# Squared-ReLU attention and an FFN on one core: the first two batches' keys in tiles of 128

## The chip, the core and the metric

The kernel runs on one core of a Trainium2 chip. Its engines are TensorE (PE in the profile), VectorE (DVE), ScalarE (ACT), GpSimd (POOL) and SyncE (SP, which here only starts DMAs). Each works through its own queue in order; semaphores tie the queues together. Sixteen DMA engines move data. The metric is the device time of one execution in microseconds (us), as a median of several runs. The kernel before takes 531.14 us (median of 6 runs, 529.06 to 533.16).

## The reference

Eight batches, twelve heads, 448 tokens, head size 64:

```python
scores = scale * q @ k.T                  # per batch and head, 448 x 448
attn   = np.maximum(scores, 0.0) ** 2 / S
x      = (attn @ v)                       # heads side by side: 448 x 768
xn     = (x - mean(x)) / sqrt(var(x) + 1e-6) * g_ln
out    = x + np.maximum(xn @ w_ch1, 0.0) @ w_ch2      # 768 -> 3072 -> 768
```

There is no softmax: a score tile is only clipped at zero and squared, so the keys of a head may be cut in any way and in any order, as long as values and scores are cut alike.

## The kernel before

Work goes by *pairs* of heads (six a batch, numbered 0 to 47 over all batches, `NPAIR` = 6). For a pair, q and k are transposed (`att_T`), so that the head dimension lies on the partitions; a score *slot* `(i, t)` is the scores of both heads of pair `i` for the `t`-th group of keys (`att_QK`, lines 241 to 268): one matmul per head into one of two PSUM buffers `sc`, one ScalarE activation (ReLU, line 268) into a bf16 tile, and one VectorE product that squares it (line 271). The value product (`att_AV`, line 278) sums over the four groups of keys, and VectorE evacuates it as xT (line 298). For batch 0 VectorE also multiplies it with the gains into xc (line 302); this is what the notes call the norm vector.

**Two layouts of keys.** Batches 2 to 7 read their keys as three groups of 128 (`NF` = 3 per partition row) and one of 64. The last 64 keys of two neighbouring pairs share one slot (line 249 on): four matmuls of 64 rows by 64 columns (line 254), each head in its half of the partitions. Values lie accordingly in `v_heads` and in `v_rest`, which is zero where the other head's keys stand. Two pairs then take seven slots. Their q and k are turned by DMA transposes that SyncE starts (line 226). Batches 0 and 1 (`PE_T` = 2) have four groups of 112 keys, eight slots for two pairs, and are transposed on TensorE (`pe_T`, line 208), since w2 and the transposing queue are not free yet.

**The order** is written out by hand. Loads of q, k, v and w1 are issued from GpSimd's queue (lines 737 to 747). Then come six `step_fine` (line 582), one for each pair of batch 0: slots, the value product of the pair before in two halves, the transposes of the next pair, the mean over features of xT (`mean_part`, line 311), and `warm_up` matmuls (line 532) on zeros. `first_end` finishes batch 0's attention and begins pair 6; `ffn_1_first` centers (line 334) and starts the first FFN product. `ffn_1_all` runs the 24 row blocks of that product (line 368), two PSUM banks in turn, and puts *excursions* between them: up to three slots of the next batch's attention, with the third slot's ReLU on VectorE (line 266) in spare banks, and one value product of a pair that is ready. For batch 0 the excursions follow the table `IN_FIRST`, the transposes `T_IN_FIRST`, the statistics of x (lines 359 to 361, on x_tok, which SyncE makes by DMA transposes in line 348) `STATS_AT`; the second entry of `STATS_AT` holds for all later batches. `ffn_2_first` is batch 0's second product (line 413): sixteen parts, tile after tile in one bank each, evacuated in line 399; between the parts stand the gains (line 314) and the centering for batch 1, `carry` (line 379) and the sums of w2 blocks (line 195). Later batches use seven block products instead of eight (`seven`, line 430, with VectorE sums in line 424 and GpSimd sums in line 464).

All loads of later batches (lines 146 to 148, 156, 160) also go through GpSimd's queue, in the order in which they are written, each as soon as the ring buffer it writes to is free.

Of the kernel before, what the change touches and what calls it, by code (L numbers as in the profile page):

```python
# [11 lines left out]
def kernel(  # L12
# [10 lines left out]
    nc = tc.nc  # L23
# [77 lines left out]
    nc.vector.memset(warm, 0.0)  # L101

# [19 lines left out]
    early = w2[:, B_SUM:].rearrange("p a k d -> p (a k d)")[:SP, :4 * EARLY]  # L122
    early = early.rearrange("p (n h e) -> p n h e", n=4, h=H)
    v1_sb = s_sb.rearrange("p a k d -> p (a k d)")[:SP, :EARLY].rearrange("p (h e) -> p h e", h=H)
    v0_sb = v_ring[:SP].rearrange("p (h e) -> p h e", h=H)
    first_qkv = {0: (early[:, 0], early[:, 1], v0_sb), 1: (early[:, 2], early[:, 3], v1_sb)}

    def load_heads(b, pieces):
        pairs = dict(zip("qkv", zip(first_qkv[b], (q, k, v))))
        for name, h0, hs in pieces:  # L130
            sb, src = pairs[name]
            nc.gpsimd.dma_start(
                sb[:, h0:h0 + hs, :],
                src[b, h0:h0 + hs].rearrange("h (p j) d -> p h (j d)", j=NJ))
# [15 lines left out]
    v_heads = v_ring[:, :H * NF * D].rearrange("p (h e) -> p h e", h=H)  # L150
    v_rest = v_ring[:, H * NF * D:].rearrange("p (a e) -> p a e", a=NPAIR)

    def load_v(i):

        b, a = divmod(i, NPAIR)
        nc.gpsimd.dma_start(v_heads[:, 2 * a:2 * a + 4],
# [6 lines left out]
    def v_of(i):  # L163
        b, a = divmod(i, NPAIR)
        return first_qkv[b][2][:, 2 * a:2 * a + 2]

    def load_early():
        q_sb, k_sb, _ = first_qkv[0]
        casts = []
        for sb, src, eng, r0, cast in ((q_sb, q, nc.sync, 0, nc.vector.tensor_copy),  # L170
                                       (k_sb, k, nc.scalar, 6, nc.scalar.copy)):
            st = h[:SP, r0:r0 + 2, :].rearrange("p a t -> p (a t)").bitcast(fp32)
            st = st[:, :2 * NJ * D].rearrange("p (h e) -> p h e", h=2)
            eng.dma_start(st, src[0, :2].rearrange("h (p j) d -> p h (j d)", j=NJ))
            casts.append((cast, sb[:, :2, :], st))
        for cast, dst, st in casts:
            cast(dst, st)
        with nc.allow_non_contiguous_dma(reason="768 gains, once"):
            nc.sync.dma_start(g_sb, moe_g_ln.rearrange("(ko kp) -> kp ko", kp=P))
# [20 lines left out]
    def bf_view(bank):  # L200
        return bank[:, :S].bitcast(bf16).rearrange("p (t s) -> p t s", t=2)

    def pe_T(i, t, ps):
        b, pr = divmod(i, NPAIR)
        sb = first_qkv[b][t]
        for j in range(NJ):
            for hh in range(2):
                nc.tensor.transpose(  # L208
                    ps[hh * D:(hh + 1) * D, t, j * SP:(j + 1) * SP],
                    sb[:, 2 * pr + hh, j * D:(j + 1) * D],  # L210
                    identity[:SP, :SP])
# [4 lines left out]

    def q_of(i, r):
        return qkT[i][r, :NJ, :SP]

    def by_j(x):  # L220
        return x.rearrange("p (j s) -> p j s", j=NJ)

    def att_T(i, copy=None):
        if i >= PE_T * NPAIR:
            new_qkT(i)
            nc.sync.dma_start_transpose(qkT[i], qk_ring[:, i % 3].rearrange("p j c -> p (j c)"))
            return
        if i == 0:
            new_qkT(0)
            for t, cp in enumerate((nc.vector.tensor_copy, nc.scalar.copy)):  # L230
                ps = bf_view(next_f())
                pe_T(0, t, ps)
                cp(qkT[0][:, t * NJ:(t + 1) * NJ, :SP], by_j(ps[:, t, :]))
# [4 lines left out]
        new_qkT(i)  # L238
        (copy or nc.vector.tensor_copy)(qkT[i][:, :, :SP], ps.rearrange("p t (j s) -> p (t j) s", j=NJ))  # L239

    def att_QK(i, t, relu_by=nc.scalar):

        full = attn_pool.tile([P, 2, S], bf16, tag="attn")
        keys = SP if i < PE_T * NPAIR else P
        at = full[:keys]
# [556 lines left out]
```

## Time and profile before

| | us |
|---|---|
| median of 6 runs | 531.14 |
| the profiled execution | 529.06 |
| its span on the core | 527.3 |
| TensorE busy in the span | 519.2 |
| VectorE / ScalarE / GpSimd busy | 377.6 / 277.0 / 217.1 |
| VectorE busy from 10 to 30 | 19.2 of 20 |
| ScalarE busy from 10 to 30 | 18.7 of 20 |
| batch 0's attention ends, centering starts | 30.05 |
| first FFN product, batch 0 | 30.79 to 70.3 |
| second FFN product, batch 0 | 70.3 to 87.1 |
| first FFN product, batch 1 / batch 2 | 87.1 to 127.4 / 155.0 to 192.8 |
| last w1 chunk / last w2 chunk landed | 53.75 / 76.88 |

In the profile a line of a timeline gives start, length, engine, source line, operation and shapes; `x2` means two instructions merged, and brackets give the idle time before them with what ended it. A matmul's length contains its way through the array, so lengths overlap: what a step costs TensorE is the distance to the next start. The chain of waits is followed back from the last instruction to what released each step. The DMA engines are busy without a gap from 4 us to 77 us, at about 200 GB/s.

### The profile page before, as it was taken

The numbers are of one execution on the slowest core, as the hardware profiler recorded it, in microseconds if no ns is written. First come the engines' busy times: TensorE is split into PE (matmuls) and PEld (weight loads), VectorE is DVE, ScalarE is ACT, GpSimd is POOL, SyncE is SP. The second block draws the span as 40 slices with busy tenths as digits, with TensorE's granted clock in tenths as the row PEclk, the third lists the DMA queues.
The fourth block names the chain that finished last, engine by engine and source line by source line (L and its number), as shares of the span: only waits on it lengthen the run. The fifth ranks groups of instructions, "written<-read, shape, count | busy, mean of one in ns | idle before, by whom it ended". The sixth has DMA issues, their size and how long they took to land.

```text
span 527.3 us, 13742 instructions
## 1 busy us (share of the span) xinstructions
PE 519.2 (98%) x5723; PEld 316.1 (60%) x5723; DVE 377.6 (72%) x667; ACT 277.0 (53%) x449; POOL 217.1 (41%) x248
## 2 busy tenths in 40 slices
PE   8999999999999999999999999999999999999996
PEld 4445566556875566655666556655666556665665
DVE  4967889695858868589684886788695876960265
ACT  6956662787227662266623666366624765234320
POOL 9425128377522665227732277228732000320021
PEclk9999999999999999999999999999999999999999
DMA  9999999999637994579924699469924300250022
GB/s 150 196 194 208 204 191 134 192 118 97 73 87 97 110 89 67 129 73 105 112 50 109 73 114 142 83 64 117 104 59 109 46 17 3 69 114 1 1 62 61
DMA packets 171246, 53.04 MB, mean 101 GB/s; under 512 B 145072, under 2 KB 171184, under 8 KB 171184
## 3 DMA queue, kind: packets, MB, share of 16 engines
q0 software_dynamic: 99744, 25.74, 53.4%
q1 hardware_dynamic: 70944, 26.03, 27.0%
q8 instruction: 44, 0.72, 0.6%
q10 hardware_dynamic: 496, 0.40, 0.2%
q14 instruction: 18, 0.15, 0.1%
HBM read 51.91 MB, written 11.01 MB: 119 GB/s over the span
## 4 chain that ended last, share of the span: by engine, by line
PE 94%; DMA 2%; ACT 2%; DVE 1%; issue 0%; DVEq 0%; ACTq 0%
PE f L368 39%; PE f L430 34%; PE f L291 7%; PE sc L259 5%; PE f L413 3%; PE f L259 1%; DMA x_tok<-xT 1%; ACT full L268 1%; PE f L208 1%; PE sc L254 1%; DMA h<-in_k_dram 1%; PE f L627 1%; PE f L532 1%; PE f L327 1%; ACT h L370 0%
## 5 line engine op out<-in xcount | busy, mean ns | idle before, releaser
L368 PE MATMUL f<-xc,w 128*64 128x448 bf16 x2256 | 227.3, 354 | 0.3
L368 PEld LDWEIGHTS <-w 128*64 128x64 bf16 x2256 | 124.9, 110 | 94.0 <-issue 19.4
L370 ACT ACTIVATE h<-f 128x448 bf16<-128x448 f32 x188 | 102.5, 545 | 99.2 <-PE f L368 97.9
L430 PE MATMUL f<-w,s_sb 128*64 128x384 bf16 (+2 forms) x1584 | 130.0, 324 | 0.0
L268 ACT ACTIVATE full<-sc 128x896 bf16<-128x896 f32 (+1 forms) x126 | 108.1, 916 | 15.2 <-PE sc L259 12.5
L430 PEld LDWEIGHTS <-s_sb 128*64 128x64 bf16 x1584 | 92.5, 110 | 34.8
L271 DVE TENSOR_TENSOR full<-full 128x896 bf16<-128x896 bf16 (+1 forms) x174 | 98.7, 617 | 6.9 <-ACT full L268 6.7
L464 POOL TENSOR_TENSOR o_t<-o_t,x_tok 128x384 f32<-128x384 f32 x26 | 24.4, 938 | 152.5 <-ACT o_t L463 132.0
L146 POOL DMA_DIRECT2D qk_ring<-in_q_dram x36 | 48.1, 1338 | 87.5 <-DMA qkT_t<-qk_ring 83.7
L266 DVE TENSOR_SCALAR full<-f 128x448 bf16<-128x448 f32 (+1 forms) x89 | 51.5, 617 | 22.1 <-PE f L259 22.1
L463 ACT ACTIVATE o_t<-f,rstd 128x384 f32<-128x384 f32 x26 | 15.1, 581 | 94.8 <-DVE acc L468 46.8
L424 DVE TENSOR_TENSOR s_sb<-h 128x1536 bf16<-128x1536 bf16 x65 | 64.8, 1013 | 0.0
L147 POOL DMA_DIRECT2D qk_ring<-in_k_dram x36 | 57.2, 1590 | 6.1 <-DMA w<-in_moe_w_ch_dram 6.1
L430 PE MATMUL f<-w,h 128*64 128x384 bf16 x624 | 52.9, 326 | 0.0
L148 POOL DMA_DIRECT2D qk_ring<-in_k_dram x36 | 49.5, 1375 | 7.4 <-DMA w<-in_moe_w_ch_dram 7.4
L298 DVE TENSOR_SCALAR xT<-f 128x448 bf16<-128x448 f32 x43 | 26.7, 622 | 28.5 <-PE f L291 26.6
L430 PEld LDWEIGHTS <-h 128*64 128x64 bf16 x624 | 36.7, 110 | 14.4
L291 PE MATMUL f<-full,v_ring 128*64 128x448 bf16 (+1 forms) x336 | 40.6, 354 | 0.7 <-DVE full L271 0.6
L464 POOL TENSOR_TENSOR acc<-acc,x_tok 128x384 f32<-128x384 f32 x24 | 28.1, 1177 | 22.8 <-ACT acc L463 21.8
L259 PE MATMUL sc<-qkT_t 64*128 64x448 bf16 (+1 forms) x228 | 35.5, 365 | 0.3 <-DVE qkT_t L239 0.2
L160 POOL DMA_DIRECT2D v_ring<-in_v_dram x36 | 33.0, 1239 | 5.2 <-DMA w<-in_moe_w_ch_dram 5.0
L334 DVE SCALAR_TENSOR_TENSOR xc<-f,g_sb,xc 128x448 bf16<-128x448 f32 x48 | 30.2, 677 | 6.0 <-PE f L327 6.0
(75 smaller groups left out, 376.8 us busy)
## 6 DMA issues: line engine op xcount, KB each, us to landing
w<-in_moe_w_ch_dram POOLq DMA_DIRECT2D x6, 768.0 KB, 23.4
w<-in_moe_w_ch_dram POOLq DMA_DIRECT2D x4, 1152.0 KB, 33.7
qk_ring<-in_q_dram POOLq DMA_DIRECT2D x36, 112.0 KB, 5.0
qk_ring<-in_k_dram POOLq DMA_DIRECT2D x36, 96.0 KB, 5.3
v_ring<-in_v_dram POOLq DMA_DIRECT2D x18, 192.0 KB, 5.1
out_dram<-o_t SPq DMA_DIRECT2D x9, 168.0 KB, 2.2
out_dram<-o_t SPq DMA_DIRECT2D x9, 144.0 KB, 2.1
out_dram<-acc SPq DMA_DIRECT2D x7, 144.0 KB, 2.1
```

The lines of the kernel that those rows point to most:

```text
L147: nc.gpsimd.dma_start(k_to[:, :NF], k[b, heads, :SF].rearrange("x (p t) d -> p t x d", t=NF))
L148: nc.gpsimd.dma_start(k_to[:SS, NF], k[b, 2 * a:2 * a + 2, SF:].rearrange("x s d -> s x d"))
L259: nc.tensor.matmul(by_j(half[hh]), qkT[i][r, NJ + t, :keys], q_of(i, r), start=True, stop=True)
L266: nc.vector.tensor_scalar(at[:, x], half[x], 0.0, None, op0=Alu.max)
L268: nc.scalar.activation(at, ps[:keys, :, :S], Act.Relu)
L271: nc.vector.tensor_mul(attn[i, t], attn[i, t], attn[i, t])
L291: nc.tensor.matmul(ps[hh * D:(hh + 1) * D, :], weights, values, start=(t == 0), stop=(t == NJ - 1))
L368: nc.tensor.matmul(ps[c * D:(c + 1) * D, :], w1[:, ki, n0:n0 + D], xc[:, ki, :], start=(ki == 0), stop=(ki == K1 - 1))
L370: nc.scalar.activation(h[:, ni, CARRY:], ps, Act.Relu)
L424: nc.vector.tensor_tensor(s_sb[:, n], x, y, op=op)
L430: nc.tensor.matmul(ps[c * D:(c + 1) * D, :d1 - d0], stat[:, ki, c * D:(c + 1) * D], w2[:, slot, ki, d0:d1], start=(start and ki == 0), sto ...
L464: nc.gpsimd.tensor_tensor(o_t, o_t, x_half(m, dh), op=Alu.add)
```

## The change

Batches 0 and 1 get the key layout of the other six: three groups of 128 and a shared slot for the last 64 keys of two pairs. Queries keep their four groups of 112. Transposes stay on TensorE. Loads split accordingly into a main part, a `k last` and a `v last`; the zeros of `v_rest` are written by VectorE at the start. `step_fine` now covers two pairs, the loads of w1 chunks 2 to 5 and of the rest of batch 1 move between the steps (`load_next`), and the numbers of warm-up matmuls differ. The product with the gains runs on GpSimd for the first four pairs of batch 0. `IN_FIRST` shrinks to six excursions of three slots behind a first one of one slot; the last value product of batch 1's attention comes before the second FFN product instead of inside it. `ffn_2_first` goes through two tiles at once, half by half. Batch 1's statistics stand at row blocks 15, 18, 21 and 23 instead of 6, 9, 12 and 15.

```diff
+    nc.vector.memset(v_ring[:, H * NF * D:], 0.0)
+    v1_sb = s_sb.rearrange("p a k d -> p (a k d)")[:, :H * NJ * D]
+    nc.vector.memset(v1_sb[:, H * NF * D:], 0.0)
...
+            elif name == "k":
+                nc.gpsimd.dma_start(first_k[b][:, heads, :NF].rearrange("p h t d -> p h (t d)"),
+                                    k[b, heads, :SF].rearrange("h (p t) d -> p h (t d)", t=NF))
+            elif name == "k last":
+                nc.gpsimd.dma_start(first_k[b][:SS, heads, NF], k[b, heads, SF:].rearrange("h s d -> s h d"))
+            elif name == "v":
+                nc.gpsimd.dma_start(v_heads[:, heads], v[b, heads, :SF].rearrange("h (p t) d -> p h (t d)", t=NF))
+            elif name == "v last":
+                for e in range(4):
+                    r0 = row0(e // 2, e % 2)
+                    nc.gpsimd.dma_start(v_rest[r0:r0 + SS, e // 2::2, r0:r0 + D],
+                                        v[b, e::4, SF:].rearrange("g s d -> s g d"))
...
         if b == 0:
-            nc.vector.tensor_scalar(xc[:, pr, :], xT_of(b, pr), g_sb[:, pr:pr + 1], None, op0=Alu.mult)
+            eng = nc.gpsimd if pr < NPAIR - 2 else nc.vector
+            eng.tensor_scalar(xc[:, pr, :], xT_of(b, pr), g_sb[:, pr:pr + 1], None, op0=Alu.mult)
...
     def step_fine(i):
+
         att_QK(i, 0)
-        if 0 < i < NPAIR - 1:
-            att_T(i + 1)
-        elif i > 0:
-            warm_up(4)
+        att_T(i + 1)
         att_square(i, 0)
         att_QK(i, 1)
         att_square(i, 1)
-        if i == 0:
-            att_T(1)
+        if i:
+            att_AV(i - 1, 0)
             warm_up(1)
         else:
-            att_AV(i - 1, 0)
+            warm_up(4)
         att_QK(i, 2)
-        if i == 0:
-            warm_up(4)
-        else:
+        if i:
             att_AV(i - 1, 1)
-        att_square(i, 2)
-        att_QK(i, 3)
-        att_square(i, 3)
-        if i > 1:
             mean_part(i - 2)
-            warm_up(2)
         else:
             warm_up(4)
+        att_square(i, 2)
+        att_QK(i, NF)
+        att_square(i, NF)
+        if i:
+            warm_up(4)
+            mean_part(i - 1)
+        else:
+            warm_up(5)
+        att_QK(i + 1, 0)
+        if i + 2 < NPAIR:
+            att_T(i + 2)
+        else:
+            warm_up(5)
+        att_square(i + 1, 0)
+        load_next()
+        att_QK(i + 1, 1)
+        att_square(i + 1, 1)
+        att_AV(i, 0)
+        warm_up(1)
+        att_QK(i + 1, 2)
+        att_AV(i, 1)
+        att_square(i + 1, 2)
+        warm_up(1)
 
     def first_end():
         i = NPAIR
+        mean_part(i - 2)
         att_AV(i - 1, 0)
         att_T(i, nc.scalar.copy)
-        mean_part(i - 2)
...
         for t in range(2):
             att_square(NPAIR, t)
+        excursion(1)
...
-    IN_FIRST = {4: 2, 6: 3, 9: 3, 12: 3, 15: 3, 18: 3, 20: 3, 22: 2}
-    T_IN_FIRST = {5: 1, 8: 2, 11: 3, 14: 4, 17: 5}
+    IN_FIRST = (5, 8, 11, 14, 17, 20)
+    T_IN_FIRST = {4: 1, 7: 2, 10: 3, 13: 4, 16: 5}
...
-    STATS_AT = ((19, 21, 23), (6, 9, 12, 15))
+    STATS_AT = {0: (18, 21, 23), 1: (15, 18, 21, 23), 2: (6, 9, 12, 15)}
...
-            for m in range(2):
-                for part in range(4):
+            for half in range(2):
+                for m, part in [(m, 2 * half + x) for m in range(2) for x in range(2)]:
                     plain_part(b, m, dh, part, 4, box)
                     if n == 1:
-                        next_AV(bank=spare[0])
...
-        load_heads(0, [("q", 2, 2), ("k", 2, 2), ("q", 4, 2), ("k", 4, 2), ("v", 0, 4), ("q", 6, 2), ("k", 6, 2),
-                       ("v", 4, 4), ("q", 8, 4), ("k", 8, 4), ("v", 8, 4)])
+        load_heads(0, [("q", 2, 2), ("k", 2, 2), ("k last", 2, H - 2), ("q", 4, 4), ("k", 4, 4), ("v", 0, 4),
+                       ("v last", 0, H), ("q", 8, 4), ("k", 8, 4), ("v", 4, 4), ("v", 8, 4)])
         load_early()
-        load_heads(1, [("q", 0, 2), ("k", 0, 2)])
+        load_heads(1, [("q", 0, 2), ("k", 0, 2), ("k last", 0, H)])
         load_w1(0)
         load_heads(1, [("q", 2, 4), ("k", 2, 4)])
         load_w1(1)
-        load_heads(1, [("q", 6, 6), ("k", 6, 6)])
-        load_heads(1, [("v", 0, H)])
-        for c in range(2, NCH):
-            load_w1(c)
+        later = [lambda: None,
+                 lambda: (load_w1(2), load_heads(1, [("v", 0, H), ("v last", 0, H)])),
+                 lambda: (load_heads(1, [("q", 6, 6), ("k", 6, 6)]), load_w1(3), load_w1(4))]
...
-        for i in range(NPAIR):
+        for i in range(0, NPAIR, 2):
             step_fine(i)
+        load_w1(5)
         first_end()
...
-        nc.gpsimd.memset(v_rest, 0.0)
```

## The prediction

> **What bounds the kernel now.** I read the page first: TensorE's row and the chain that ended last.
>
> ```profile
> PE 519.2 (98%) x5723; PEld 316.1 (60%) x5723; DVE 377.6 (72%) x667; ACT 277.0 (53%) x449; POOL 217.1 (41%) x248
> PE 94%; DMA 2%; ACT 2%; DVE 1%; issue 0%; DVEq 0%; ACTq 0%
> ```
>
> TensorE (PE) holds 94% of the chain, so an instruction taken off another engine is worth only what it takes out of a wait of TensorE. The change works on the first 130 us, so I then read the timeline of that stretch, all engines, columns start, length, engine, line.
>
> ```profile
> 14.45 0.57 PE L291 MATMUL f<-full,v_ring 112*64 112x448 bf16 x4
> 14.95 0.40 PE L259 MATMUL sc<-qkT_t 64*112 64x448 bf16 x2
> 15.27 0.57 PE L291 MATMUL f<-full,v_ring 112*64 112x448 bf16 x4
> 15.77 0.40 PE L259 MATMUL sc<-qkT_t 64*112 64x448 bf16 x2
> 16.10 0.36 PE L311 MATMUL f<-xT,ones 128*128 128x448 bf16 x1
> 16.30 0.38 PE L532 MATMUL f<-w,ones 128*128 128x256 bf16 x2
> 16.61 0.40 PE L259 MATMUL sc<-qkT_t 64*112 64x448 bf16 x2
> 16.94 0.58 PE L208 MATMUL f<-identity,w 112*64 112x112 bf16 x16
> 17.45 0.40 PE L259 MATMUL sc<-qkT_t 64*112 64x448 bf16 x2
> ```
>
> One pair of batch 0 takes 3.33 us (13.28, 16.61, 19.95, 23.28), always in the same steps: a score slot 0.33 to the next start, half a value product 0.50, sixteen transposes 0.51, a mean with two warm-ups 0.51. Steps that never vary are no waits. ScalarE is full on the page, but each of its activations starts 0.44 after its score slot's matmuls (14.95, then 15.38), while two back to back start 0.80 apart: it waits for TensorE, with 0.03 to spare. VectorE runs all but gapless from 9.24 to 28.5 and falls back by 0.24 a pair (3.57 against 3.33), which its buffers absorb until the last pair. So TensorE's own work sets this stage, and VectorE its end.
>
> Next the chain in time around batch 1, and SyncE's queue:
>
> ```profile
> 95.00 6.53 DMA x_tok<-xT
> 101.60 0.57 DVE stats L360
> 104.75 0.57 PE f L291 x4
> 105.65 0.38 PE sc L254 x2
> ```
> ```profile
> 78.55 9.73 SPq L226 DMA_TRANSPOSE qkT_t<-qk_ring  x3
> 88.33 7.88 SPq L348 DMA_TRANSPOSE x_tok<-xT  x6
> 96.31 5.54 SPq L392 DMA_DIRECT2D out_dram<-o_t  x8
> 102.22 22.70 SPq L226 DMA_TRANSPOSE qkT_t<-qk_ring  x6
> ```
>
> VectorE waits in a statistics instruction for x_tok until 101.5, and TensorE's second half of a value product comes 0.83 late. But 0.9 later comes a second wait: the score matmuls of pair 14's shared slot (line 254) need pair 15's transposed keys, which SyncE asks for at 102.22, behind the same transposes and eight stores, and which land at 105.61. That queue starts when pair 12's last key piece lands (78.41), 1.5 after the last w2 chunk (76.88). It is a clock of the DMAs, not of TensorE.
>
> **First stage.** Three score slots fewer: 3 x 0.33 = -1.0. The shared slot has the form of line 254, whose step (94.00 to 94.32) is 0.32 like any other. The transposes move the same columns (6x128 + 2x64 = 8x112). Warm-ups: 27 matmuls before, 36 after, 0.11 each (four 0.54, two 0.31, halved): +1.0. Means and warm-ups now stand in 18 groups instead of 11; a group put between two others adds one change of tile shape, 0.09 to 0.14 by the remainders above: 7 x 0.12 = +0.85. Waits: 0.09 and 0.19 in pair 0, about 0.35 before the last value product and 0.20 at the last mean, 0.8 in all. After, the mean of pair 4 follows that pair's value product with one warm-up between; it needs the evacuation (0.62 and some 0.15 at each end), so 0.65 of wait, and the last mean keeps its 0.20. Sum of the stage: +0.85. Its bounds: 0 (no cost for the changes of shape) and 1.9 (if pair 1's keys, whose last rows are the third DMA, land 1.0 later than the slot order asks; the load now in that place landed at 6.29, the transposes come at 6.85).
>
> Four norm-vector products leave VectorE (0.25 of its queue each), which lies behind TensorE. GpSimd has no such product in the trace. Its nearest rows are two-operand sums of 384 columns, 0.91 alone. They tell what it does to VectorE:
>
> ```profile
> 142.41 3.06 POOL L464 TENSOR_TENSOR acc<-acc,x_tok 128x384 f32<-128x384 f32 x2 [0.77 <-ACT acc L463]
> 142.16 2.54 DVE L424 TENSOR_TENSOR s_sb<-h 128x1536 bf16<-128x1536 bf16 x2
> L424 DVE TENSOR_TENSOR s_sb<-h x65: 927/948/1675, 128.4 to 518.4; 128x1536 bf16<-128x1536 bf16 x65
> ```
>
> Two GpSimd sums beside two VectorE sums of 0.95 stretch these to 2.54. So a product costs VectorE between 0 and 0.7, net -0.25 to +0.45. The first two start once GpSimd has issued the second w1 chunk (about 16), where VectorE, relieved of 0.25 and of half a square (0.27) a pair, absorbs them. The other two stand behind six more DMA issues; a DMA issue here waits until the eighth one before it has landed (30.49 for 30.21, 33.03 for 32.75), so they come after batch 1's second q load (24.05), at 25 to 27, beside the last squares: 0 to 1.4 on the path, I take 0.35. They still end 3 us before the first centering (30.05 + 0.85). Stage with this: +1.2.
>
> [...]
>
> **Batch 0's first FFN half.** 19 slots instead of 22 lie here. Slots by the step of their excursion: before 2 x 0.52 + 6 x 0.705 = 5.27; after 0.33 + 3 x 0.705 + 3 x 0.80 = 4.84 (0.80 is the one at 94.00). -0.43, and one entry less: -0.48. The twelfth value product only moves from the second half to here.
>
> **Batch 0's second FFN half.** The parts (0.975 each, 10.72 over 11) now go through both banks at once. The six centerings are put into VectorE's queue after the fifth part; bank one is full after the sixth, and the ninth needs it back.
>
> ```profile
> 76.62 3.64 DVE L334 SCALAR_TENSOR_TENSOR xc<-f,g_sb,xc 128x448 bf16<-128x448 f32 x6 [0.81 <-PE f L327]
> 80.18 0.61 DVE L399 SCALAR_TENSOR_TENSOR o_t<-f,rstd,x_tok 128x384 f32<-128x384 f32 x1
> ```
>
> From the fifth part's end (75.96 here): centerings start at +0.66, the evacuation behind them ends at +4.83; TensorE arrives after 0.38 of means and three parts, +3.30. Wait: +1.5. Today that evacuation stands ahead of the centerings (75.19) and the next lands in a bank not wanted for 4 us. Bounds 0 and 1.6.
>
> **Batch 1.** Statistics later: -0.83; the later wait for pair 15 (0.40) falls away only because TensorE comes later. Their four places at the end put 1.25 us each on VectorE, which idles there (1.85 at 126); the sums of the next half are asked for 3.9 us later.
>
> TensorE's sum: +1.2 - 0.48 + 1.5 - 0.83 - 0.40 = +1.0.
>
> **The DMA clock** under it. Up to the last w2 chunk the queue never empties, so what counts is the sum. 46 heads of k and v now come as 112 rows of 512 B, 0.30 a head by landings (1.19 to 1.26 for four heads): 13.8. The new main part is the form of batch 2's v, four heads 0.95 after the load before it: 11.0. Of the last rows there are 46 x 64 = 2944. By the 768-row key loads (0.65) 2.5; by the 128-row ones (0.16 to 0.24) 4.6; I take 3.1, nearer the first, since most come in loads of 640 and 768. Clock: +0.3, bounds -0.3 and +1.8; by packets without overlap (2024 of them filled 216% of 2 us on 16 engines, 34 ns each) 6.3, so +3.5. It decides only beyond +1.0.
>
> [...]
>
> **Total.** Profiled execution 529.06 (span 527.29 and 1.8 around it) + 1.0 = 530.1; the median of the runs, 531.14, lies 2.1 above it: **532.1**. From batch 2 on TensorE's work is as before, so the shift stays.
>
> **Rivals.** *A, faster:* VectorE, not TensorE, paces the first stage. For: it has no gap there and falls back. Its period would go from 3.57 to about 3.05, five pairs, -2.6, and the stage's +1.2 is gone: -2.6 - 0.48 + 1.5 - 1.23 = -2.8, **528.3**. Against: the fixed steps of TensorE. *B, slower:* the small rows cost their packet time, w2 and the queue behind it come 3.5 later, and TensorE stands at line 254 until 109.1: **534.6**; from +1.0 on. Against: long runs of such rows overlapped (0.65 for 768). [...] *D, the wait of 1.5 isn't there:* TensorE's sum would be -0.5, and the DMA clock decides with +0.3, 531.4: the same band.
>
> **Numbers.** About 0.5% (2.7 us) is what can be told from no change. Forecast with D 0.57, A 0.12, B 0.18, C 0.13. Parts of B and C stay within the bound and part of A too, while unforeseen waits are likelier than gains: faster 0.10, same 0.57, slower 0.33. The range 529.4 to 535.6 cuts off A's far end and what lies over B.
>
> **What would show it.** In the changed profile: score slots of batch 0 still in fixed steps of TensorE, ScalarE with gaps; centering starting about 1 us later than 30.05; an idle stretch of 1.5 of TensorE before the ninth part, ended by line 399's instruction; no statistics on the chain near 101; line 254's second step at 106 to 107. Wrong if the first stage ends before 29, if TensorE stands for keys of pair 15 past 108, or if pieces of the first stage wait for k or v.

## The result and the profile after

The changed kernel takes 535.68 us (median of 33 runs, 532.19 to 538.38), the kernel before, run beside it, 532.72 (70 runs, 529.04 to 535.42). The ratio is 1.0056, with a 95% interval of 1.0041 to 1.0070: slower by 3.0 us, where +1.0 was forecast, and just past the top of the range. The profiled execution took 532.83 (span 531.0; before 529.06 and 527.3).

The page of the changed kernel, in the same two rows:

```profile
PE 521.0 (98%) x5732; PEld 317.4 (60%) x5732; DVE 378.7 (71%) x660; ACT 273.9 (52%) x443; POOL 228.5 (43%) x259
PE 81%; DMA 12%; POOL 3%; ACT 2%; issue 1%; DVE 0%; POOLq 0%; DVEq 0%; ACTq 0%
```

TensorE is as full as before, and 1.8 us more of it is work or longer matmuls. The chain of waits now has 12% DMA and 3% GpSimd in it where it had 2% and none, but this row must not be taken at its word: the chain, followed back, leaves TensorE at 82.11, at an evacuation that it puts down to a load landed at 81.69, and stays among loads up to the start; VectorE, which makes that evacuation, was busy with other work until it began (shown below). At the place that matters, the shared slot near 108, the chain stays on TensorE. So where the time comes in is read from the start of each stage on TensorE (us from the start of the span):

| | before | after | shift |
|---|---|---|---|
| first FFN product of batch 0 starts | 30.79 | 32.39 | +1.60 |
| second FFN product of batch 0 starts | 70.33 | 73.02 | +2.69 |
| first FFN product of batch 1 starts | 87.06 | 90.57 | +3.51 |
| shared slot of pair 14, its first two matmuls | 105.25 | 107.87 | +2.62 |
| the same, its second two (pair 15's keys) | 105.65 | 108.30 | +2.65 |
| the slot after it | 105.96 | 108.60 | +2.64 |
| second FFN product of batch 1 starts | 127.36 | 130.11 | +2.75 |
| last w2 chunk landed | 76.88 | 80.03 | +3.15 |
| pair 15's keys landed | 105.61 | 108.25 | +2.64 |

From 130 us on the shift stays at 2.7 until the last stores; the end of this one execution adds 1.0 (span +3.7). The value product that now comes ahead of the second FFN product (it lay inside it) puts 0.76 of the second row's shift into that row and takes it out of the next. The two last rows are as important as the rest: TensorE and the DMAs arrive at the shared slot within 0.4 us of each other, as they did before. First the slot in the changed kernel, as TensorE's timeline and in the chain, then the same form in the kernel before where no key was late, then SyncE's queue in the changed kernel:

```profile
107.87 0.80 PE L279 MATMUL sc<-qkT_t 64*64 64x448 bf16 x4
108.60 0.36 PE L284 MATMUL sc<-qkT_t 64*128 64x448 bf16 x2
```
```profile
107.19 0.76 PE f L314 x8
107.94 0.31 PE sc L279 x2
108.25 0.04 issue
108.30 0.38 PE sc L279 x2
```
```profile
94.00 0.38 PE L254 MATMUL sc<-qkT_t 64*64 64x448 bf16 x4
94.32 0.36 PE L259 MATMUL sc<-qkT_t 64*128 64x448 bf16 x2
```
```profile
81.83 8.70 SPq L253 DMA_TRANSPOSE qkT_t<-qk_ring  x3
90.59 8.00 SPq L372 DMA_TRANSPOSE x_tok<-xT  x6
98.68 6.12 SPq L416 DMA_DIRECT2D out_dram<-o_t  x8
104.97 21.53 SPq L253 DMA_TRANSPOSE qkT_t<-qk_ring  x6
```

Where no key is late, the four matmuls of a shared slot start within 0.01 us of each other and the next slot follows 0.32 after them (94.00 to 94.32). Here the other two began 0.42 after the first two, when pair 15's keys had landed at 108.25. With the keys in place TensorE would have gone on to the next slot at 108.19 (107.87 and one step of 0.32) and not at 108.60: it stands 0.41, and before the change it stood 0.40. So neither of the two, TensorE's longer way or the later keys, is *the* cause: by these numbers TensorE's way alone would have put the next slot 2.2 later (108.19 against 105.96), the keys alone 2.6. VectorE is off the path there, its statistics come after it, as forecast. SyncE's queue is the old one, 2.3 to 3.3 later from its first request on.

Three more places of the changed kernel. First TensorE in pair 0 and 1 of batch 0 (columns: start, length, engine, line, operation, tile shapes, count):

```profile
6.63 0.36 PE L284 MATMUL sc<-qkT_t 64*128 64x448 bf16 x2
6.92 0.70 PE L229 MATMUL f<-identity,w 112*64 112x112 bf16 x16
7.56 0.36 PE L284 MATMUL sc<-qkT_t 64*128 64x448 bf16 x2
...
9.23 0.38 PE L279 MATMUL sc<-qkT_t 64*64 64x448 bf16 x4
9.55 0.72 PE L556 MATMUL f<-w,ones 128*128 128x256 bf16 x5
```

The sixteen transposes of a pair cost 0.64 from their start to the next (6.92 to 7.56), against 0.51 before (16.94 to 17.45 in the lines shown of before); the slot of 64 keys costs 0.32, as assumed. Beside the first FFN product the difference is larger, 0.61 instead of 0.395, here of the changed kernel and of the kernel before:

```profile
38.48 0.68 PE L229 MATMUL f<-identity,w 112*64 112x112 bf16 x16
39.09 1.33 PE L392 MATMUL f<-xc,w 128*64 128x448 bf16 x12
```
```profile
38.49 0.56 PE L208 MATMUL f<-identity,w 112*64 112x112 bf16 x16
38.88 1.30 PE L368 MATMUL f<-xc,w 128*64 128x448 bf16 x12
```

(A merged row names the shape of its first instruction; of the sixteen transposes of the changed kernel eight are 112x112, six 128x128 and two 64x64.) Then VectorE at the end of that stage, and TensorE and VectorE in the second FFN product of batch 0:

```profile
27.41 0.61 DVE L321 TENSOR_SCALAR xT<-f 128x448 bf16<-128x448 f32 x1
28.06 1.23 DVE L326 TENSOR_SCALAR xc<-xT,g_sb 128x448 bf16<-128x448 bf16 x1
29.21 0.64 DVE L295 TENSOR_TENSOR at<-at 128x896 bf16<-128x896 bf16 x1
30.51 0.62 DVE L321 TENSOR_SCALAR xT<-f 128x448 bf16<-128x448 f32 x1 [0.66 <-PE f L314]
31.17 0.34 DVE L326 TENSOR_SCALAR xc<-xT,g_sb 128x448 bf16<-128x448 bf16 x1
```
```profile
26.93 3.21 POOL L326 TENSOR_SCALAR xc<-xT,g_sb 128x448 bf16<-128x448 bf16 x2
```
```profile
78.27 3.09 PE L437 MATMUL f<-w,h 128*64 128x384 bf16 x36
82.77 7.99 PE L437 MATMUL f<-w,h 128*64 128x384 bf16 x96 [1.41 <-DVE o_t L423]
```
```profile
78.55 3.64 DVE L358 SCALAR_TENSOR_TENSOR xc<-f,g_sb,xc 128x448 bf16<-128x448 f32 x6 [3.62 <-PE f L351]
82.11 1.13 DVE L423 SCALAR_TENSOR_TENSOR o_t<-f,rstd,x_tok 128x384 f32<-128x384 f32 x2
```

VectorE's own gain product, 0.34 when alone (31.17), takes 1.23 at 28.06 while GpSimd's two last ones run (26.93 to 30.14). And TensorE stands 1.41 before the ninth part, ended by the evacuation behind the six centerings, which fill VectorE without a gap up to it: the forecast wait of 1.5.

### The profile page after: what moved, and what is told of

It is laid out like the page before. It is cut to its first block, busy times and chain, and to the rows that moved or that the text cites. A ratio compares the mean times of both kernels' runs of the same rounds, so it can differ in the third digit from the quotient of the medians.

```text
span 531.0 us, 13760 instructions
## 1 busy us (share of the span) xinstructions
PE 521.0 (98%) x5732; PEld 317.4 (60%) x5732; DVE 378.7 (71%) x660; ACT 273.9 (52%) x443; POOL 228.5 (43%) x259
## 4 chain that ended last, share of the span: by engine, by line
PE 81%; DMA 12%; POOL 3%; ACT 2%; issue 1%; DVE 0%; POOLq 0%; DVEq 0%; ACTq 0%
PE f L392 35%; PE f L454 33%; DMA qk_ring<-in_k_dram 5%; PE f L314 5%; DMA s_sb<-in_v_dram 3%; PE sc L284 3%; DMA w<-in_moe_w_ch_dram 2%; PE f L437 2%; PE f L284 1%; DMA w<-in_q_dram 1%; ACT at L292 1%; PE sc L279 1%; POOL xc L326 1%; POOL w L144 1%; POOL w L201 0%
## 5 line engine op out<-in xcount | busy, mean ns | idle before, releaser
L292 ACT ACTIVATE at<-sc 128x896 bf16<-128x896 f32 x120 | 104.6, 916 | 16.9 <-PE sc L284 12.5
L295 DVE TENSOR_TENSOR at<-at 128x896 bf16<-128x896 bf16 x168 | 96.5, 619 | 6.5 <-ACT at L292 5.9
L166 POOL DMA_DIRECT2D qk_ring<-in_q_dram x36 | 46.4, 1288 | 85.9 <-DMA qkT_t<-qk_ring 81.2
L290 DVE TENSOR_SCALAR at<-f 128x448 bf16<-128x448 f32 x89 | 51.5, 617 | 23.6 <-PE f L284 23.6
L167 POOL DMA_DIRECT2D qk_ring<-in_k_dram x36 | 55.1, 1529 | 4.6 <-DMA w<-in_moe_w_ch_dram 4.6
L168 POOL DMA_DIRECT2D qk_ring<-in_k_dram x36 | 46.2, 1283 | 5.8 <-DMA w<-in_moe_w_ch_dram 5.7
L314 PE MATMUL f<-at,v_ring 128*64 128x448 bf16 x336 | 40.2, 354 | 0.3 <-DMA v_ring<-in_v_dram 0.2
L284 PE MATMUL sc<-qkT_t 64*128 64x448 bf16 x206 | 31.3, 356 | 0.0
```

The costliest lines, as they stand in the source:

```text
L166: nc.gpsimd.dma_start(q_to, q[b, heads].rearrange("x (p j) d -> p j x d", j=NJ))
L167: nc.gpsimd.dma_start(k_to[:, :NF], k[b, heads, :SF].rearrange("x (p t) d -> p t x d", t=NF))
L284: nc.tensor.matmul(by_j(half[hh]), k_of(i, r, t, P), q_of(i, r), start=True, stop=True)
L290: nc.vector.tensor_scalar(at[:, x], half[x], 0.0, None, op0=Alu.max)
L292: nc.scalar.activation(at, ps[:, :, :S], Act.Relu)
L295: nc.vector.tensor_mul(attn[i, t], attn[i, t], attn[i, t])
```

## The experiments

Ratios are against the kernel before, run on the same chip beside each kernel; an interval is about 0.003 to each side, so that 1.5 us can just be told apart. Four groups were run beside each other: 1 to 4, 5 to 8, 9 and 10, 11 to 14; 15 stood alone. Between groups ratios are compared, not medians, since the kernel before had 531.14 to 533.16 in them. Times of single events are from the one profiled execution of each, and such times scatter: in seven kernels with the same first stage the first FFN product starts anywhere from 31.75 to 32.85. "Kernel 1" is the kernel of run 1, and so on. What a TensorE row gives in brackets counts from the end of the row before it; at the shared slot TensorE loses 0.37 more than that, since all four matmuls could have started together.

**1. Tile after tile.** The changed kernel with the second FFN product of batch 0 in the order of before.

```diff
-            for half in range(2):
-                for m, part in [(m, 2 * half + x) for m in range(2) for x in range(2)]:
+            for m in range(2):
+                for part in range(4):
```

> The changed kernel with the parts of batch 0's second product back in the order tile after tile. Theory of two clocks: TensorE's own path and SyncE's queue reach pair 14's shared slot within 0.1 us of one another (108.19 and 108.25), so the 1.4 us of idle before the ninth part goes, but TensorE then waits for pair 15's keys: its step stays at 108.2 to 108.3 and the total at +2.9 against the kernel before (the changed kernel: +3.0). Rival 'TensorE's path alone': the step comes at 106.7 to 106.9 and the total is +1.5. Rival 'DMA clock alone': as the theory here, +2.9.

536.0, ratio 1.0066 [1.0035, 1.0098]. The stage takes 15.98 instead of 17.55, so the wait is gone; but TensorE, now at the shared slot at 106.32, stands there. TensorE's timeline in this kernel:

```profile
106.32 0.38 PE L279 MATMUL sc<-qkT_t 64*64 64x448 bf16 x2
108.62 0.38 PE L279 MATMUL sc<-qkT_t 64*64 64x448 bf16 x2 [1.93 <-DMA qkT_t<-qk_ring]
```

(The 108.19 of the expectation is where TensorE would have begun the next slot; its second two matmuls could have begun at 107.88, so the two clocks were 0.4 apart and not 0.1.) TensorE reaches the slot 1.55 sooner than in the changed kernel and passes it 0.32 later (108.62 against 108.30), held by a DMA: TensorE's way is not alone in setting the time.

**2 and 3. Token transposes later.** To take that second wait away, batch 1's six token transposes go behind pair 15's keys; in 2 with the new order of parts, in 3 with the old.

```diff
+            if b == 1 and ni == 5:
+                for ki in range(K1):
+                    ffn_x(1, ki)
             ffn_1(ni)
```

> The changed kernel with the six transposes that make x_tok of batch 1 issued after pair 15's transposes (row block 5 of batch 1's first product) instead of before them. SyncE then asks for pair 15's keys at about 98 instead of 104.97 and they land by 102. Theory of two clocks: TensorE's own path stands behind, so the step still comes at 108.1 to 108.2 and the total stays within 0.2 of the changed kernel's +3.0. Rival 'DMA clock alone': the step comes 2.5 earlier (105.6) and the total is +0.4. Rival 'TensorE's path alone': +3.0, as the theory.

> Both of the two edits before. Theory of two clocks: only now does the time move, by the 1.5 of idle before the ninth part: step at 106.6 to 106.8, total +1.4 against the kernel before. Rival 'TensorE's path alone': +1.5, but then the order of the parts alone has given it already. Rival 'DMA clock alone': +0.4 or less, given already by the late x_tok alone.

536.2, 1.0080 [1.0050, 1.0110], and 537.17, 1.0088 [1.0056, 1.0120]. Both expectations missed. The keys came sooner (104.6 in 2), but the edit made a wait of its own, as ScalarE's timeline of run 2 shows:

```profile
105.45 0.54 ACT L319 ACTIVATE xT<-f 128x448 bf16<-128x448 f32 x1 [2.90 <-DMA x_tok<-xT]
```

Tiles are 128 tokens and a batch is 448, so batch 1's token tiles begin with 64 tokens of batch 0, whose half of xT the evacuation of pair 12 overwrites: it has to wait for the transposes. These runs say nothing on the theory.

**4. The kernel before with late statistics alone.**

```diff
-    STATS_AT = ((19, 21, 23), (6, 9, 12, 15))
+    STATS_AT = {0: (19, 21, 23), 1: (15, 18, 21, 23), 2: (6, 9, 12, 15)}
```

> The kernel before with one part of the change: batch 1's statistics at row blocks 15, 18, 21 and 23. Theory (the wait for pair 15's keys is set by the DMAs): the idle stretch of 0.64 before the value product at 104.75 goes, the second step of pair 14's shared slot stays at 105.6, and the total is 0 to -0.1. Rival (the statistics alone held TensorE): step at 104.8, total -0.8.

531.39, 0.9998 [0.9954, 1.0043]. From the start of batch 1's first product to the shared slot TensorE needs 17.47 instead of 18.19; then this kernel's TensorE stands:

```profile
105.08 0.38 PE L254 MATMUL sc<-qkT_t 64*64 64x448 bf16 x2
107.11 0.38 PE L254 MATMUL sc<-qkT_t 64*64 64x448 bf16 x2 [1.66 <-DMA qkT_t<-qk_ring]
```

The gain of 0.72 (0.83 forecast) is there in this stage and eaten by the next wait.

**5. Stores later.** Kernel 1, the eight stores of batch 0's product behind pair 15's keys (row block 5 of batch 1).

```diff
-            store(o_t, m, dh * HD, (dh + 1) * HD)
+            late_stores.append((o_t, m, dh * HD, (dh + 1) * HD))
```

> The changed kernel with FFN-2 of batch 0 tile after tile, and the eight stores of that product asked for only at row block 5 of batch 1's first product, behind pair 15's key transposes: SyncE no longer stands at the stores (98.7 to 104.8) before it asks for pair 15's keys. Theory of two clocks: these transposes start about 98.7 instead of 105.3 and land by 106; TensorE reaches the shared score slot of pair 14 at about 106.3 and its second pair 0.4 later, instead of at 108.6, and the total falls by about 2 against the same kernel with early stores: 1.002 to 1.003 of before. Rival, TensorE's own way alone sets the time or the transposes wait for something else: keys as late as 108.6, total as it was, 1.0066.

532.6, 1.0025 [1.0000, 1.0050]. The keys are asked for at 99.36 and land at 107.28, not 106, behind the token transposes (the last landed at 104.69); TensorE stands 0.36 at the slot instead of 1.93. The ratio fell to what the theory says, with nothing changed on TensorE, though the two intervals still touch (run 1's begins at 1.0035).

**6. No small rows.** Kernel 1 without the loads of the last 64 keys and values that GpSimd asks for; it leaves these keys and values out of the computation.

```diff
             elif name == "k last":
-                nc.gpsimd.dma_start(first_k[b][:SS, heads, NF], k[b, heads, SF:].rearrange("h s d -> s h d"))
+                nc.vector.memset(first_k[b][:SS, heads, NF], 0.0)
...
             elif name == "v last":
+                pass
```

> The changed kernel with FFN-2 of batch 0 tile after tile, and without the loads of the last 64 keys and values of batches 0 and 1 that GpSimd asks for (those operands are zeros instead; they are left out of the computation). Theory, small rows cost the queues their time: the last piece of w2 lands at about 76.5 to 77.5 instead of 79.4, x_tok and pair 15's keys follow 2 to 3 earlier, TensorE stands at the shared slot of pair 14 at 106.5, and the total falls by about 2: 1.002 to 1.003. Rival, the weights land late for another reason (the order in which GpSimd asks for them, its work on the norm vector): w2 lands at 79.4 again and the total stays 1.0066.

530.67, 0.9979 [0.9954, 1.0005]. The last w2 chunk lands at 77.00 instead of 79.37, the keys at 106.92, TensorE stands 0.26 at the slot. The small rows cost the DMA clock at least 2.4 (every kernel with them has its last w2 chunk at 79.37 or later). But 77.00 is also where the kernel before has it (76.88; 77.32 in run 4), although kernel 6 has 2944 rows of 128 B less to load, by estimate 1.8 us at the 205 GB/s named below: the main loads of 128 rows, forecast to gain 2.8, gained nothing here.

**7. Whole-row transposes.** Kernel 5, the last keys transposed over 128 rows, 64 of them zeros.

```diff
-            rows = SP if t == 0 else P if j < NF else SS
+            rows = (SP, P)[t]
```

> The kernel with late stores, and the transposes of the last 64 keys of batches 0 and 1 made over all 128 rows (64 of them zeros), so that TensorE never changes the shape of its tile in them. Theory, the 64-row transposes cost a change of shape of 0.1 to 0.2 each: a pair's transposes take 0.52 instead of 0.62 in the first stage and 0.40 instead of 0.61 in batch 0's first product; the first product ends some 1.6 sooner than with late stores alone, and the total falls by up to 1.6, as far as pair 15's keys let it. Rival, the transposes are longer because of the 128 rows or of their waits: same durations, same total.

530.95, 1.0008 [0.9977, 1.0040]. A pair's transposes take 0.545 in the first stage (0.636 with 64 rows, 0.514 before) and 0.424 in the first FFN product (0.611 and 0.395). The second FFN product starts at 71.13 instead of 72.78 in run 5: 1.65 sooner, for 1.6 expected. In this execution it goes no further: TensorE comes to the slot at 104.51 and stands 2.22 for pair 15's keys. Whether it reaches the end in the others can't be told: the median is 1.65 below that of run 5, within the intervals, and the profiled execution (533.28) is one of the three longest of the ten.

**8. The norm vector on VectorE.** Kernel 5 with one line of before.

```diff
-            eng = nc.gpsimd if pr < NPAIR - 2 else nc.vector
+            eng = nc.vector
```

> The kernel with late stores, and batch 0's norm vector (its six products xc) on VectorE, as before, instead of GpSimd. Theory, GpSimd's products take 1.8 each and hold VectorE's own product for 1.23 instead of 0.34 at the end of the first stage: centering starts 0.5 to 0.9 sooner, and the total falls by as much. Rival, GpSimd's help is worth what it was put there for: four products of 0.34 more on VectorE, which is behind in the first stage, and centering starts 0.5 to 1.4 later.

531.85, 1.0019 [0.9991, 1.0046]. VectorE's fifth product takes 0.34 again, and the first FFN product starts at 31.83 instead of 32.16: 0.33 sooner, less than expected. That is less than the scatter of this start, but two more pairs that differ by this line alone point the same way (0.32 in run 14 against 12, 0.17 in run 15 against 6): GpSimd's help seems to cost a little more than it saves. In this run the late stores stood ahead of pair 16's key transposes, and TensorE lost 1.96 there.

**9 and 10. Token transposes first.** In SyncE's queue ahead of the keys of pairs 12 to 14; in 9 on kernel 1, in 10 on kernel 4.

```diff
             if PE_T * NPAIR <= i + 3 < NP_ALL:
+                if i < PE_T * NPAIR:
+                    kept.append(i)
+                    return
                 att_T(i + 3)
...
                             ffn_x(1, ki)
+                        for i in kept:
+                            att_T(i + 3)
+                            loads.append(i + 6)
```

> The changed kernel with FFN-2 of batch 0 tile after tile, and SyncE asking for batch 1's six token transposes (line 372) before the key transposes of pairs 12 to 14 (line 253) instead of behind them: xT of batch 1 is ready at 72 to 73, and the keys of pair 12 come only behind the last piece of w2, at 81, so SyncE stood with the token transposes behind it for 8 us. Theory of two clocks: the token transposes are asked for at 73 to 82, the keys of pairs 12 to 14 follow, the stores start at 90 and pair 15's keys are asked for at about 97 and land by 103; TensorE has no wait at the shared slot of pair 14 (first pair 106.3, second 106.7) and the total falls by about 1.9 against the same kernel without this: 1.003 of before. Rival, the token transposes beside the loads of w2 delay its last piece past 82.5, where the second half of FFN-2 of batch 0 needs it: TensorE stands there, and the total stays at 1.006 or rises.

> The kernel before with batch 1's statistics late and with the same order of SyncE's requests (batch 1's token transposes ahead of the key transposes of pairs 12 to 14). Theory of two clocks: with late statistics alone TensorE came to the shared slot of pair 14 at 105.08 and stood there until pair 15's keys landed at 107.07; with the keys 4 or more us earlier it goes on at 105.5, so the gain of the late statistics shows: 1.5 less than with late statistics alone, 0.997 of before. Rival, the gain of late statistics is lost in another place (VectorE's queue later in batch 1): total as before, 1.000.

534.55, 1.0060 [1.0031, 1.0089], and 532.36, 1.0000 [0.9972, 1.0027]. The wait at the slot is gone in both, but the rival of run 9 holds: SyncE, no longer held up by the keys, asked for the token transposes from 47 us on (42 in run 10), each as soon as its pair was ready, and beside them w2 came 6.5 later than in run 1 (in run 10 at 84.10, 6.8 later than in run 4). So run 10 has the total of its rival, but for another reason than the rival gave. TensorE in run 9:

```profile
85.94 4.38 PE L437 MATMUL f<-w,h 128*64 128x384 bf16 x51 [2.17 <-DMA w<-in_moe_w_ch_dram]
```

**11 to 14. Token transposes in SyncE's gap.** Behind pair 13's keys, ahead of pair 14's, for whose load SyncE stood 5 us; nothing but pair 14 is kept back. Run 11 is kernel 1 with it, 12 adds the whole-row transposes, 14 these and the norm vector on VectorE; 13 is kernel 4 with it. Against 9 and 10 one line differs:

```diff
-                if i < PE_T * NPAIR:
+                if i == PE_T * NPAIR - 1:
```

> The changed kernel with FFN-2 of batch 0 tile after tile, and SyncE asking for the key transposes of pairs 12 and 13, then for batch 1's six token transposes, and only then for pair 14's keys, for whose load SyncE stood from 84 to 89. Theory of two clocks: w2's last piece lands at 79.4 as without this edit, the token transposes are asked for at 84 to 92, pair 14's keys at 92 (they are needed at 101), pair 15's at 98 or 99 and they land by 104; TensorE does not stand at the shared slot of pair 14 (first pair 106.3, second 106.7), and the total falls by 1.9: 1.003 of before. Rival, the transposes beside the loads of pairs 14 and 15 slow each other and the same bytes come no sooner: pair 15's keys at 107 or later, total 1.005 or more.

> The same with the transposes of the last 64 keys made over all 128 rows. Theory: TensorE's way to the shared slot is 1.6 shorter (104.7), and the keys allow it: total 1.000 of before. Rival, pair 15's keys land after 104.7: the total falls by less, by as much as they let it.

> The kernel before with batch 1's statistics late and the same order of SyncE's requests. Theory: TensorE comes to the shared slot at 105.1 and goes on at 105.5 without a wait, 1.6 sooner than with late statistics alone: 0.997 of before. Rival, the late statistics gain nothing: 1.000.

> The changed kernel tile after tile, with the requests in that order, whole-row transposes, and batch 0's norm vector on VectorE. Theory: 0.3 less than without the last of these (what late stores with VectorE's norm vector showed): 0.9995 of before; the fewer score slots of batch 1 gain about as much as the first stage still loses. Rival, the first stage is longer by VectorE's four more products: 1.002.

| run | median | ratio, interval | last w2 chunk | TensorE stands for keys |
|---|---|---|---|---|
| 11 | 532.06 | 0.9988 [0.9968, 1.0008] | 80.62 | 0.50 (pair 14) and 0.78 (pair 15) |
| 12 | 531.28 | 0.9982 [0.9957, 1.0007] | 81.75 | 1.89 (pair 14) |
| 14 | 531.66 | 0.9988 [0.9967, 1.0009] | 81.31 | 1.20 and 1.09 |
| 13 | 529.74 | 0.9949 [0.9929, 0.9970] | 78.38 | none |

Run 13 is the clean case. SyncE and TensorE in it:

```profile
80.06 3.03 SPq L226 DMA_TRANSPOSE qkT_t<-qk_ring  x2
83.15 9.23 SPq L348 DMA_TRANSPOSE x_tok<-xT  x6
92.59 1.24 SPq L226 DMA_TRANSPOSE qkT_t<-qk_ring  x1
```
```profile
105.87 0.38 PE L254 MATMUL sc<-qkT_t 64*64 64x448 bf16 x4
106.18 0.36 PE L259 MATMUL sc<-qkT_t 64*128 64x448 bf16 x2
```

The four matmuls of the slot start together, the next slot follows 0.31 later, and the keys have been there since 104.31. Late statistics and the order of requests are worth 0.5% together; the order alone was not run on the kernel before, so the share of each is not shown. This version beats both kernels. Runs 11, 12 and 14 are the counterpart: up to the second FFN product of batch 0 TensorE's way is 0.85 shorter in 12 than in 11 (71.52 instead of 72.37) and 1.17 in 14, and the total does not move by what can be told: w2 lands 2.2 to 3.4 later than in run 13, pair 15's keys at 107.1 to 107.4 instead of 104.3, and TensorE stands for keys. Against run 1 (1.0066) the order of requests brought run 11 some 4 us by the ratios; the two traces show 1.3 of it (batch 1's second product at 129.09 instead of 130.43), and the rest is not traced: run 1's profiled execution, 532.71, was the shortest of its ten.

**15. No small rows and the norm vector on VectorE,** to see what became of the gain forecast for the main loads (the expectation calls them the larger loads). It is kernel 6 with the one line of run 8.

> The changed kernel tile after tile, without GpSimd's loads of the last 64 keys and values of batches 0 and 1 (zeros instead; they are left out of the computation), and with batch 0's norm vector on VectorE. Theory, the larger loads do gain some 2 us, and in e6 GpSimd's products held the requests back: the DMAs move 190 GB/s and more from 25 to 40 us, the last piece of w2 lands at 74 to 75.5 instead of 77.0, and TensorE has no wait at the shared slot of pair 14; total 0.5 to 1 below e6, 0.9965. Rival, the larger loads gain nothing: w2 at 77 again, and the total as in e6, 0.998.

530.92, 0.9969 [0.9943, 0.9995]; w2 at 76.32, and TensorE has no wait at the slot. The time is between the two expectations. w2 lands 0.7 sooner than in run 6, but whether GpSimd's products held requests back is not shown: the same line moved w2 0.4 sooner in run 14 against 12 and 1.4 later in run 8 against 5. Of the forecast 2.8 no more than about 1 is there (76.88 and 77.32 in runs with the loads of before).

What the DMAs moved, by stretches (last two columns: DMA share, GB/s), in the kernel before and in the changed one:

```profile
10.00:20.00 10.00, 10.00 (x108) 4.37 (x108) 9.81 (x20) 9.93 (x13) 7.03 (x9) 1.00 1.33 190
20.00:30.00 10.00, 9.77 (x91) 4.29 (x91) 9.37 (x19) 8.78 (x11) 2.46 (x3) 1.00 1.32 194
30.00:40.00 10.00, 9.16 (x81) 5.00 (x81) 6.22 (x11) 5.48 (x10) 3.91 (x4) 1.00 1.37 196
40.00:50.00 10.00, 10.00 (x126) 5.76 (x124) 7.66 (x14) 6.40 (x10) 5.69 (x5) 1.00 1.24 207
```
```profile
10.00:20.00 10.00, 9.83 (x107) 4.21 (x104) 8.92 (x16) 9.03 (x11) 9.48 (x12) 1.00 1.67 149
20.00:30.00 10.00, 9.30 (x92) 4.10 (x90) 8.60 (x14) 7.61 (x9) 8.96 (x9) 1.00 1.29 193
30.00:40.00 10.00, 8.98 (x73) 4.47 (x74) 6.41 (x12) 5.25 (x9) 2.62 (x4) 1.00 1.45 184
40.00:50.00 10.00, 10.00 (x124) 5.48 (x120) 7.28 (x14) 6.51 (x10) 8.35 (x7) 1.00 1.41 199
```

In three of the four stretches the DMAs are busier, and in all four they move less: (190 - 149 + 194 - 193 + 196 - 184 + 207 - 199) x 10 us = 620 KB, which at the 205 GB/s of 50 to 70 us are 3.0 us, the 3.15 by which w2 is late. Two thirds of it lie from 10 to 20, where the last values of batch 0 and the last keys of batch 1 are loaded. Without these loads that stretch moved 194 (run 6), but the two after it only 174 and 178, and 174 and 190 in run 15. Why the DMAs slow down there, beside batch 0's token transposes, was not found out.

## Why the prediction was wrong

The main reading, TensorE's path and a clock of the DMAs that meet at pair 14's shared slot, held. Two sizes failed, one on each of the two, and by the numbers at the slot either alone would have made TensorE go on there 2.2 (its own way) or 2.6 (the keys) later.

- **"The transposes move the same columns (6x128 + 2x64 = 8x112)"**, at no cost: this is the step on TensorE's side that failed. The columns are the same; the shapes are not. A pair costs 0.12 more in the first stage (five pairs, and 0.10 for a sixth) and 0.22 more in the first FFN product (five pairs): 0.7 + 1.1 = 1.8. Run 7, whole rows with more columns, gives 0.09 and 0.19 of it back per pair, so it is the 64-row transposes, not the columns. Whether the price is that of the change of shape or of a 64-row transpose itself, no run separates. The prediction put a price on a change of shape between groups of matmuls (0.12 each, its estimate) and none on the shapes within one. These 1.8 are more than the 1.2 by which TensorE came later to the slot's first two matmuls than forecast (2.62 against 1.39, its sum without the 0.40); the other terms together were 0.6 too high, or the execution scatters by it.
- **First stage, +1.2:** +1.60 in the profiled execution; over the profiles of seven kernels that have this stage unchanged the first FFN product starts at 32.32 on average, over four with that of before at 31.15, +1.17. The sum was right by luck, since its parts were not: what was measured holds 0.7 for the transposes that was not in it. The mean's wait of 0.65 was 0.56. GpSimd's products were forecast to hold VectorE up by 0.35; beside them VectorE's own fifth product took 1.23 instead of 0.34, and taking GpSimd's help away gained 0.33 in run 8.
- **First FFN half of batch 0, -0.48:** +1.09, of which 0.76 is the value product moved here, so +0.33, which is 0.81 more than forecast. The transposes' 1.1 covers it.
- **Second half, wait of 1.5:** the stage is 1.58 longer once the value product is set aside, and run 1 takes 1.57 out. Right; rival D is out.
- **Statistics, -0.83:** 17.30 instead of 18.19 from the start of batch 1 to the slot, -0.89; run 4 -0.72. Right.
- **"The later wait for pair 15 (0.40) falls away only because TensorE comes later":** it did not fall away (TensorE stands 0.41 there, 0.40 before), since the keys came later too. The -0.40 of the sum is thus a term that failed with the DMA clock.
- **The DMA clock, +0.3, bounds -0.3 and +1.8:** measured +3.15 at w2 and +2.64 at the keys. The price of the small rows (3.1) was about right, run 6 shows 2.4 of it at least; what failed is the other term, "four heads 0.95", 11.0 in place of 13.8: the values of batch 0, four heads a load, did land 0.89 to 1.04 apart instead of 1.2, but the end of the queue came no sooner for it (run 6). The forecast's +0.3 without the 2.8 is +3.1, which is what was measured. The term was a sum of times of single loads, and the rates show that the stretch as a whole did not get faster. The rejected bound of +3.5, by packets without overlap, was the nearest number, but for another reason than the one that showed.
- **Rivals:** B had the mechanism and the place, TensorE at line 254 with the keys of pair 15, at 109.1 by its count and at 108.25 by the trace; it decides "from +1.0 on", and TensorE itself came 2.62 later, so the wait there is only the 0.41. It grows as soon as TensorE's part is mended (run 1). C, a slower first stage through GpSimd's products, did not show: without these products the stage ends no more than 0.33 sooner (run 8). A is out: the score slots stay in fixed steps of TensorE.
- **Signs of being wrong:** two of the three that the prediction named did show. TensorE stands for keys of pair 15 past 108 (until 108.30), and a piece of the first stage waits for v, for 0.17 at 11.66.

Of the distance to the forecast (535.68 against 532.1) 2.0 are this. The other 1.6 are the level: the kernel before, run beside it, has its median at 532.72, not at 531.14.

What stays open: the changed kernel with its own order of parts and nothing but earlier keys was not run, so that TensorE's way alone would have cost 2.2 is read from the trace and not shown by a run; and what slows the DMAs from 20 to 40 us in runs 6 and 15 was not settled.

## What to carry over

Where two independent chains arrive at one instruction within half a microsecond, work out both with the same care: taking 1.6 us out of one gives nothing while the other stands, and the gain of a right edit (late statistics, 0.7 in their stage) was lost in the next wait until the second chain was moved too (0.5% for both). Look at the shapes inside a group of matmuls and not only at their columns (the 64-row transposes cost 0.12 and 0.22 a pair), and measure a queue's speed as bytes over a stretch, not as a sum of single loads (of 2.8 summed up, no more than about 1 was there). Before moving a request forward in a queue, ask what held it back until then: behind the keys SyncE's token transposes could not meet the w2 loads, ahead of them they did, and w2 landed 6.5 later (run 9).

## What the runs showed of the hardware

In four of these traces a stop of TensorE was followed by a stretch at half the granted clock. After the 1.89 in run 12 the next three row blocks took 5.28 instead of 3.60 (run 11), and the granted clock was 0.50 for the 3.41 us that follow; runs 3 (after a stop of 4.46), 7 (after its 2.22) and 10 (after one of 2.54) each show one such stretch of 3.41. (The end of every execution, when TensorE has nothing left to do, is not counted here.) After 1.93 in run 1 and 2.17 in run 9 the clock stayed at 1.00. TensorE's timeline in run 12, and three stretches of 3.41 (the column ahead of the last two is the granted clock):

```profile
101.94 0.36 PE L286 MATMUL sc<-qkT_t 64*128 64x448 bf16 x2 [1.89 <-DMA qkT_t<-qk_ring]
102.43 5.28 PE L394 MATMUL f<-xc,w 128*64 128x448 bf16 x36
```
```profile
99.06:102.47 3.41, 1.52 (x16) 0.48 (x14) 0.15 (x1) 2.00 (x4) 0.00 (x1) 1.00 1.70 186
102.48:105.88 3.40, 3.40 (x22) 1.65 (x22) 3.32 (x5) 1.76 (x3) 2.83 (x3) 0.50 1.35 277
105.89:109.30 3.41, 3.41 (x38) 1.64 (x36) 0.35 (x2) 1.84 (x4) 1.33 (x2) 1.00 1.48 135
```

The length of the stop does not tell these cases apart; the idle share of a window of a fixed grid does. All four stretches at 0.50 begin a whole number of 3.41 us after the trace's first change of the clock (28 of them in run 12, 30 in 3 and 7, 23 in 10). Cut on that grid, TensorE was idle for 1.89 (run 12), 2.22 (7), 2.54 (10) and 2.90 us (3) of the window ahead of the half clock, and while matmuls still went on no window of the seventeen traces without one after it was idle for more than 1.84. That 1.84 is run 9, whose 2.17 lies across two windows, as does run 1's 1.93 (1.31 and 0.63).

In run 4 the times of the executions go with the clock: of its ten, with a stop of 1.66 in the profiled one, six had a mean granted clock of 0.998 or more and took 529.73 to 531.54, and four, with 0.997 or less, 534.98 to 536.82; one window at half clock is 0.003 of this mean.

GpSimd's product of a 128x448 bf16 tile with a column of factors took 1.4 to 1.9 us in the changed kernel, VectorE's 0.34 when alone.
